# Building the second-level factors of w_out from row-block pairs in the first token group, instead of from reloaded quarters in groups 1 and 2

## The chip, the core and the metric

The kernel runs on one core of a Trainium2 chip. The metric is the time of one execution of the whole program on the device, in microseconds (us), and the median of several runs is compared. The engines of a core run side by side, each in its own program order, and meet through semaphores: TensorE (PE) multiplies, VectorE (DVE) and ScalarE (ACT) work element by element, GpSimd (POOL) and SyncE (SP) here do little but issue DMA transfers, which 16 DMA engines carry out.

## The reference, cut to what matters

```python
B, H, S, D = 4, 8, 768, 64                      # attention, blocks of 64 positions
intra = einsum('bhic,bhjc->bhij', qb, kb) * Dmask
out[:, :, sl] = einsum('bhij,bhjd->bhid', intra, vb) + einsum('bhid,bhde->bhie', qb * lam_pow, kv_state)
kv_state = lam_block * kv_state + einsum('bhsd,bhse->bhde', kb * rev_pow, vb)
...
x = out.transpose(0, 2, 1, 3).reshape(3072, 512)
h = x @ w_in                                    # 512 x 2048
g = h - np.tanh(h)
return (g @ w_out).astype(np.float32)           # 2048 x 512
```

The weights reach the kernel as 64-bit floats, q, k and v as 32-bit floats. It rounds the weights to 32-bit floats itself, block by block.

## The kernel before

**Tokens and weights.** Six groups (g = 0 to 5) of 512 tokens pass through attention, the product with `w_in` (`up`), the function g = h - tanh(h) and the product with `w_out` (`down`). The matrices are cut in halves both ways, and from group 1 on a product of two such 2x2 block matrices is made by Strassen's scheme in Winograd's form, with 7 products in place of 8: product n (1 to 7) multiplies one sum of blocks of g by one factor, which is a block of `w_out` or a sum of blocks. The seven factors are B11, B21, B22 and T1 to T4. Each of the seven can be cut a second time in the same way: its 16 matmuls of 128x256 columns ("plain", function `down`, line 655) become 7 times 4 matmuls of 128x128 columns ("twice", function `down_twice`, line 708). The set `TWICE = (3, 5, 6, 4, 7)` names the products that are made twice; each needs the seven sub-factors of its factor, again blocks and sums of blocks, now of 128 columns.

**Where the factors live.** `w_out` has 16 row blocks of 128 rows. Row blocks kt and kt + 8 form pair kt (kt = 0 to 7). In group 0, `round_block` rounds the two 64-bit blocks of a pair (three ACT instructions, then a shift and an add on DVE, lines 279 to 284), and `sums_out(kt)` makes T1, T2, T3 and T4 of the pair (lines 255 to 258) and writes all seven factors to a DRAM tensor `factors`. The sub-factors live in a second DRAM tensor, `fine`, with 5 factors times 7 sub-factors. Those sub-factors that are plain blocks (numbers 1, 2 and 3) are copied there by `sums_out` too. A sum sub-factor adds rows of pair 2u to rows of pair 2u + 1.

**The first group.** Group 0 does its `down` plainly by pairs: `down_first(kt)` makes 14 matmuls for the seven products of pair kt, into seven PSUM accumulators that stay open over all eight pairs. While pair kt is multiplied, pair kt + 1 is summed and pair kt + 3 is rounded into the buffer that pair kt leaves (three buffers in turn: two tiles `wt`, and the tensors `ws[3]` and `ws[2]`). `sums_late(kt)` overwrites two blocks of g with their sums, between products 1, 2 and the other five. Raw 64-bit blocks are loaded by POOL's queue into four buffers (`WAHEAD = 4`), so a load waits until an earlier raw block has been rounded.

**The sums of the sub-factors, before.** They are made in groups 1 and 2. `load_quarters(t)` reads four quarters of a factor back from `factors`, `factors_twice(t)` makes the four sums (lines 602 to 604) and writes each to `fine`. Factors of products 5 and 6 are made in group 1's `up`, those of 4, 7 and 3 in group 2's `up`. So in group 1 products 4, 7 and 3 are plain (line 550). The quarters of group 2 pass through the same ring of seven buffers `wb` (`RING = 7`) that brings the factors of all products, in the order of the list `stream`.

**What sets the order.** Each engine carries out its instructions in the order that a scheduler gives them, and those marked with `tc.keep_in_program_order` (or `tied`) keep the order of the text among themselves. A DMA that POOL issues waits in POOL's own queue, and all that stands behind it waits too. SP loads q, k and v; for group 2 on it loads q and k in 16 small transfers each (`load_blocks`, line 143), and the first of these waits until the last raw block has been rounded, since its buffer takes the place of the raw blocks.

Of the kernel before, what the change touches and what calls it, by code (L numbers as in the profile page):

```python
# [24 lines left out]
def kernel(  # L25
# [154 lines left out]

    NX = 7
    factors = dram.tile([NX, 128, KH, 256], F32, name="factors")

# [38 lines left out]
    def weights(n):  # L222

        while ready["done"] < min(n, len(blocks)):
            at_ = ready["done"]
            load_weights(at_ + WAHEAD)
            kind, n_, m = blocks[at_]
            if kind == "out" and m == 0:
                pair[n_] = pair_tiles(n_)
            w = w1[n_][:, m] if kind == "in" else pair[n_][0][:, 2 * m:2 * m + 2]  # L230
            if at_ in wraw:
                round_block(w, wraw.pop(at_), at_ < 2 * KI)
            else:
                load_block(nc.gpsimd, w, kind, n_, m)
            ready["done"] += 1

    def pair_tiles(kt):

        if kt % 3 == 2:
            return tuple(ws[u].rearrange("p x k c -> p (x k) c")[:, 0:4] for u in (3, 2))  # L240
        wt = wst.tile([128, 8, 256], F32, name="wt", tag="w")
        return wt[:, 0:4], wt[:, 4:8]

# [7 lines left out]
    def sums_out(kt):  # L251
        bt, tt = pair[kt]
        b11, b12, b21, b22 = (bt[:, x] for x in range(4))
        t1, t2, t4, t3 = (tt[:, x] for x in range(4))
        nc.vector.tensor_tensor(t1, b12, b11, op=AL.subtract)
        nc.vector.tensor_tensor(t2, b22, t1, op=AL.subtract)
        nc.vector.tensor_tensor(t3, b22, b12, op=AL.subtract)
        nc.vector.tensor_tensor(t4, b21, t2, op=AL.subtract)
        f = factors[:].rearrange("x p k c -> p x k c")
        nc.gpsimd.dma_start(out=f[:, 0:1, kt, :], in_=bt[:, 0:1, :])  # L260
        nc.gpsimd.dma_start(out=f[:, 1:3, kt, :], in_=bt[:, 2:4, :])
        nc.gpsimd.dma_start(out=f[:, 3:NX, kt, :], in_=tt[:, 0:4, :])

        for x, j in ((1, 0),) if kt % 2 == 0 else ((2, 0), (3, 1)):
            dst = fine[:, SUB.index(x), :, kt // 2, :].rearrange("n p c -> p n c")
            nc.gpsimd.dma_start(out=dst[:, 0:1], in_=bt[:, 3:4, ts(j, 128)])
            nc.gpsimd.dma_start(out=dst[:, 1:5], in_=tt[:, 0:4, ts(j, 128)])

    def round_block(w, raw64, first):
# [12 lines left out]

        tied(first, nc.vector.tensor_scalar(out=wb, in0=wb, scalar1=3, scalar2=None, op0=AL.logical_shift_left))
        nc.vector.tensor_tensor(wi, wi, add, op=AL.add)  # L284

# [263 lines left out]
    def twice(g, n):  # L549
        return n in TWICE and not (g == NG - 1 and n == 3) and not (g == 1 and n in (4, 7, 3))  # L550

# [7 lines left out]
    def pieces_of(g):  # L559
        if g >= GI:  # L560
            yield from ((g, ("in", 4), x) for x in (6, 5, 3))
        if g == 2:
            yield from ((g, ("quarter", t), x) for t in (2, 3, 4) for x in range(4))
        for n in (1, 2, 4, 5, 6, 7):
            yield from ((g, n, x) for x in (SUB if twice(g, n) else range(NU)))
        if g == NG - 1:
            yield from ((g, 3, x) for x in range(NU))
            return
        for kind, x in in_turn(g):
            if kind == "down":  # L570
                yield g, 3, x
            elif x in (3, 5, 6):
                yield g + 1, ("in", 2), x
# [3 lines left out]

    MADE = (5, 6, 4, 7, 3)
    quarters = {}

    def quarter_source(t, i, j):
        return factors[XAT[FACT[MADE[t]][1]]].rearrange("p (u m) c -> p u m c", m=2)[:, :, i, ts(j, 128)]

    def load_quarters(t):

        for i in range(2):
            for j in range(2):
                if t > 1:
                    quarters[t, i, j] = piece(2, ("quarter", t), 2 * i + j).rearrange("p m (v c) -> p (m v) c", v=2)
                    continue  # L590
                if t == 0:
                    x = late["pool"].tile([128, NU, 128], F32, name="wq", tag="wb", bufs=RING)
                else:
                    x = opool.tile([128, NU, 128], F32, name="oq", tag="o")
                nc.gpsimd.dma_start(out=x, in_=quarter_source(t, i, j))
                quarters[t, i, j] = x

    def factors_twice(t):

        b11, b12, b21, b22 = (quarters.pop((t, i, j)) for i in range(2) for j in range(2))  # L600
        t1, t2, t4 = (late["pool"].tile([128, NU, 128], F32, name=f"wt{x}", tag="sums", bufs=4) for x in (1, 2, 4))
        for x, dst, a, b in ((5, t1, b12, b11), (6, t2, b22, t1), (7, b12, b22, b12), (4, t4, b21, t2)):
            tc.keep_in_program_order(nc.vector.tensor_tensor(dst, a, b, op=AL.subtract))
            nc.gpsimd.dma_start(out=fine[TWICE.index(MADE[t]), SUB.index(x)], in_=dst)
            yield

    def piece(g, n, x):

        i = stream.index((g, n, x))
        while sent["n"] < min(i + RING, len(stream)):  # L610
            g_, n_, x_ = stream[sent["n"]]
            t = late["pool"].tile([128, 2, 256], F32, name="wb", tag="wb", bufs=RING)
            if isinstance(n_, tuple) and n_[0] == "quarter":
                nc.gpsimd.dma_start(out=t.rearrange("p m (v c) -> p (m v) c", v=2),
                                    in_=quarter_source(n_[1], *divmod(x_, 2)))
            elif isinstance(n_, tuple):
                nc.gpsimd.dma_start(out=t.rearrange("p m c -> p (m c)"), in_=fine_in[
# [157 lines left out]
    ACC = {1: ("ya", 1), 2: ("w", 1), 5: ("z", 1), 6: ("yb", 1), 7: ("att", 4), 4: ("att", 4), 3: ("att", 4)}  # L775
    FIRST = {1: (11, 0, 0), 2: (21, 0, 2), 3: (21, 0, 3), 4: (22, 1, 2), 5: ("S1", 1, 0), 6: (11, 1, 1), 7: (12, 1, 3)}

# [5 lines left out]
    def down_first(kt, ns):  # L783

        u, m = divmod(kt, 2)
        for n in ns:
            if kt == 0:
                acc[n] = bank("acc", *ACC[n]).rearrange("q (m c) -> q m c", m=2)
            c, part, x = FIRST[n]
            a, b = hidden(0, c)[:, u, m], pair[kt][part][:, x]  # L790
            for r in range(2):
                nc.tensor.matmul(out=acc[n][:, r, :], lhsT=a[:, ts(r, 128)], rhs=b, start=kt == 0 and r == 0,  # L792
                                 stop=kt == KH - 1, skip_group_check=True)

    def sums_late(kt):
        u, m = divmod(kt, 2)
        g11, g21, s1 = (hidden(0, c)[:, u, m] for c in (11, 21, "S1"))
        nc.vector.tensor_tensor(g11, s1, g11, op=AL.subtract)
        nc.vector.tensor_tensor(g21, g21, g11, op=AL.subtract)

    def first_results():
        flat = {n: t.rearrange("q m c -> q (m c)") for n, t in acc.items()}
        q, o11, q5, o12 = (otile(x) for x in ("q1", "o11", "q5", "o12"))
        nc.scalar.activation(q, flat[1], AF.Copy)
        nc.vector.tensor_tensor(o11, q, flat[2], op=AL.add)
        store(0, 11, o11)
        nc.vector.tensor_tensor(q, q, flat[6], op=AL.add)
        nc.vector.tensor_tensor(q5, q, flat[5], op=AL.add)
        nc.vector.tensor_tensor(q, q, flat[7], op=AL.add)
        nc.vector.tensor_tensor(o12, q5, flat[3], op=AL.add)  # L810
        store(0, 12, o12)
        nc.vector.tensor_tensor(q, q, flat[4], op=AL.add)
        store(0, 21, q)
        nc.vector.tensor_tensor(q5, q5, flat[7], op=AL.add)
        store(0, 22, q5)
# [58 lines left out]
    weights(NU * KI + 6)  # L874
    run(p1[4:])
    for kt in range(KH):
        down_first(kt, (1, 2))
        if kt + 1 < KH:
            sums_out(kt + 1)
        sums_late(kt)  # L880
        down_first(kt, (5, 4, 7, 6, 3) if kt + 1 < KH else (5, 6, 7, 4, 3))
        if kt + 3 < KH:
            weights(ready["done"] + 2)
        if kt == 2:
            sums_in(1)
# [5 lines left out]

    turns = {1: (0, ((0, 7), (1, 14))), 2: (7 * NU, ((2, 1), (3, 5), (4, 9)))}
    made, making = [], {}
    load_quarters(0)
    load_quarters(1)
    up(1, 0, 1)
    for g in range(1, NG):
        last = g == NG - 1
        p0, p1 = attention(g + 1) if not last else ([], [])
        for u in range(NU):  # L900
            for n in (2, 6, 5, 7, 1, 4, 3) if g < GI else (1, 7, 3) if u == 0 else (6, 5, 1, 7, 3) if u + 1 < NU else (
# [7 lines left out]
                if g == 1 and u < 2 and n == 5:  # L909
                    sums_in(u + 2)  # L910
                if g in turns:
                    made.append(n)
                    step = len(made) - turns[g][0]
                    for t, first in turns[g][1]:
                        if step == first:
                            if t > 1:
                                load_quarters(t)
                            making[t] = factors_twice(t)
                        if first <= step < first + 4:
                            next(making[t])  # L920
            if g == GI - 1:
# [68 lines left out]
```

## Time and profile before

| what | value |
|---|---|
| runs | 670.99, 670.28, 668.80 us; median 670.28 us |
| profiled execution, its own time | 669.39 us |
| its span, first to last instruction | 667.6 us |
| PE busy in the span | 655.6 us (98%), 4920 matmul records |
| DVE, ACT, POOL busy | 466.4, 213.7, 210.8 us |
| group 0's `down` (98.53 to 147.0 us) | PE busy all of it, DVE 30.5 us, DMA busy share 0.81 |
| group 1's `up` and `down` | 147.0 to 263.4 us |
| group 2's `up` and `down` | 263.4 to 369.7 us |
| DMA through POOL's queue | 96.49 MB, 45.0% of 16 engines' span |

A matmul on 32-bit data leaves two records in the trace, so "x32" in a line of the PE timeline is 16 matmuls. A record's duration overlaps its neighbours', so the time of a stretch is read from the start of one row to the start of the next. In a timeline, the columns are start (us from the span's start), duration, engine, line, operation, output<-inputs, shape, count, and in brackets the idle time before and what ended it.

### The profile page before, as it was taken

How to read it: one execution, taken by the hardware profiler on the slowest of the kernel's cores; microseconds unless marked ns; L12 is line 12 of the kernel's file. 1: busy time of each engine (PE TensorE's matmuls, PEld its weight loads, DVE VectorE, ACT ScalarE, POOL GpSimd, SP SyncE). 2: the span in 40 equal slices, each digit the busy share in tenths (PEclk: the TensorE clock that was granted, in tenths of full speed). 3: DMA queues.
4: the chain of work that ended last, by engine and by line, in shares of the span. 5: the costliest groups of instructions: out<-in, count | busy, mean ns of one | idle time of the engine just before them, and what ended most of it. 6: DMA issues, size and time to landing. Idle time of an engine off the chain costs nothing.

```text
span 667.6 us, 13061 instructions
## 1 busy us (share of the span) xinstructions
PE 655.6 (98%) x4920; PEld 594.1 (89%) x4920; DVE 466.4 (70%) x839; ACT 213.7 (32%) x402; POOL 210.8 (32%) x365
## 2 busy tenths in 40 slices
PE   7899999999999999999999999999999999999998
PEld 6688888888888989888999988999988899988897
DVE  4467896746988762599885379987368877357753
ACT  4787935503321112341112343112233112234110
POOL 0001445734522433254436101344300245400251
PEclk9999999999999999999999999999999999999999
DMA  9999988958855977568889533698730677610495
GB/s 209 223 201 261 286 306 234 342 160 233 229 133 137 235 188 205 150 198 259 239 260 280 142 76 75 170 274 255 215 70 17 158 237 219 219 37 0 120 295 170
DMA packets 163038, 128.82 MB, mean 193 GB/s; under 512 B 134176, under 2 KB 135328, under 8 KB 162976
## 3 DMA queue, kind: packets, MB, share of 16 engines
q0 software_dynamic: 29296, 96.49, 45.0%
q1 hardware_dynamic: 133536, 31.50, 24.0%
q8 instruction: 39, 0.64, 0.4%
q14 instruction: 23, 0.19, 0.1%
q10 hardware_dynamic: 144, 0.00, 0.0%
HBM read 103.55 MB, written 24.38 MB: 192 GB/s over the span
## 4 chain that ended last, share of the span: by engine, by line
PE 79%; issue 9%; DMA 5%; POOL 2%; SPq 2%; ACT 1%; DVE 1%; DVEq 0%; POOLq 0%; ACTq 0%
PE y L446 12%; PE y L708 10%; PE acc L792 7%; PE zw L708 7%; PE h L763 7%; PE z L446 7%; PE w L655 4%; PE y L655 4%; PE y L530 4%; PE plain L655 3%; PE sp L340 3%; PE op L394 3%; PE z L530 2%; DMA wb<-fine 2%; PE op L388 1%
## 5 line engine op out<-in xcount | busy, mean ns | idle before, releaser
L620 POOL DMA_DIRECT2D wb<-fine x147 | 79.4, 541 | 113.7 <-PE y L708 50.6
L623 POOL DMA_DIRECT2D wb<-factors x56 | 30.4, 543 | 155.9 <-PE y L655 99.7
L454 ACT ACTIVATE th<-g 128x512 f32<-128x512 f32 x76 | 47.7, 632 | 99.1 <-DVE g L459 33.2
L446 PE MATMUL y<-xt,w 128*128 128x256 f32 x320 | 74.0, 380 | 0.0
L446 PEld LDWEIGHTS y<-xt,w 128*128 128x128 f32 x320 | 59.9, 190 | 8.5 <-ACT g L534 0.9
L711 ACT ACTIVATE q<-y 128x128 f32<-128x128 f32 x84 | 23.3, 278 | 130.8 <-PE y L708 130.0
L455 DVE TENSOR_TENSOR g<-g,th 128x512 f32<-128x512 f32 x76 | 51.9, 688 | 16.8 <-ACT th L454 16.7
L763 PE MATMUL h<-xt,w 128*128 128x256 f32 x256 | 58.0, 383 | 2.3 <-DVE w L284 2.3
L763 PEld LDWEIGHTS h<-xt,w 128*128 128x128 f32 x256 | 47.7, 190 | 10.2 <-DVE w L284 2.6
L708 PE MATMUL y<-wb,g 128*128 128x128 f32 x384 | 51.1, 278 | 0.0
L708 PEld LDWEIGHTS y<-wb,g 128*128 128x128 f32 x384 | 46.4, 192 | 1.1 <-issue 0.3
L446 PE MATMUL z<-tt,ws 128*128 128x256 f32 x160 | 38.0, 380 | 0.0
L446 PE MATMUL z<-xt,ws 128*128 128x256 f32 x160 | 37.9, 380 | 0.0
L446 PE MATMUL y<-tt,ws 128*128 128x256 f32 x160 | 37.8, 379 | 0.0
L655 PE MATMUL y<-wb,g 128*128 128x256 f32 x160 | 35.6, 379 | 0.7 <-DVE g L465 0.7
L655 PE MATMUL w<-wb,g 128*128 128x256 f32 x160 | 35.8, 382 | 0.0
L344 DVE TENSOR_TENSOR ss<-sp,mask 128x512 f32<-128x512 f32 x48 | 31.1, 684 | 6.3 <-PE sp L340 6.3
L205 POOL DMA_DIRECT2D raw<-in_moe_w_out_dram x16 | 8.8, 549 | 84.7 <-ACT r L281 66.2
L655 PEld LDWEIGHTS y<-wb,g 128*128 128x128 f32 x160 | 30.3, 190 | 5.1 <-PE y L446 1.0
L446 PEld LDWEIGHTS z<-xt,ws 128*128 128x128 f32 x160 | 30.3, 190 | 4.3 <-ACT g L462 0.2
L655 PEld LDWEIGHTS w<-wb,g 128*128 128x128 f32 x160 | 30.1, 190 | 4.4
L708 PE MATMUL zw<-wb,g 128*128 128x128 f32 x256 | 33.8, 275 | 0.0
(198 smaller groups left out, 1349.6 us busy)
## 6 DMA issues: line engine op xcount, KB each, us to landing
wb<-fine POOLq DMA_DIRECT2D x147, 256.0 KB, 4.0
wb<-factors POOLq DMA_DIRECT2D x68, 256.0 KB, 4.2
raw<-in_moe_w_out_dram POOLq DMA_DIRECT2D x16, 512.0 KB, 5.8
v_nat<-in_v_dram SPq DMA_DIRECT2D x24, 256.0 KB, 5.2
fine<-wt POOLq DMA_DIRECT2D x24, 256.0 KB, 4.7
wb<-fine_in POOLq DMA_DIRECT2D x24, 256.0 KB, 4.2
k_nat<-in_k_dram SPq DMA_DIRECT2D x20, 256.0 KB, 4.9
raw<-in_moe_w_in_dram SPq DMA_DIRECT2D x8, 512.0 KB, 6.5
```

What stands on the lines that cost most here:

```text
L344: tied(g == 0, nc.vector.tensor_tensor(ss[:, j], sp[j], mask[:, j], op=AL.mult))
L446: nc.tensor.matmul(out=t[:, m, :], lhsT=wt[:, kt, ts(m, 128)], rhs=x[:, kt, :], start=first and m == 0 and kt == 0, stop=kt == 1, skip_gro ...
L454: nc.scalar.activation(th, src, AF.Tanh)
L455: nc.vector.tensor_tensor(dst(c), src, th, op=AL.subtract)
L530: nc.tensor.matmul(out=dst[:, ts(u, 128)], lhsT=a, rhs=b, start=x in (1, 2, 5) and u == 0, stop=True, skip_group_check=True)
L620: nc.gpsimd.dma_start(out=t.rearrange("p m c -> p (m c)"), in_=fine[TWICE.index(n_), SUB.index(x_)].rearrange("p u c -> p (u c)"))
L623: nc.gpsimd.dma_start(out=t, in_=factors[XAT[FACT[n_][1]]][:, 2 * x_:2 * x_ + 2, :])
L655: nc.tensor.matmul(out=t[:, m, :], lhsT=a[:, u, kt, ts(m, 128)], rhs=wb[:, kt, :], start=first and u == 0 and m == 0 and kt == 0, stop=u = ...
L708: nc.tensor.matmul(out=dst, lhsT=a[:, u, :], rhs=wb[:, ts(u, 128)], start=x in (1, 2) and u == 0, stop=u == NU - 1, skip_group_check=True)
L711: nc.scalar.activation(keep, dst, AF.Copy)
L763: tied(u == 0, nc.tensor.matmul(out=hm[c][:, m, :], lhsT=w1[u][:, i, a, ts(m, 128)], rhs=xt[0, t][:, i, :], start=m == 0 and i == 0, stop= ...
L792: nc.tensor.matmul(out=acc[n][:, r, :], lhsT=a[:, ts(r, 128)], rhs=b, start=kt == 0 and r == 0, stop=kt == KH - 1, skip_group_check=True)
```

## The change

Nothing changes in what is computed: the same 35 sub-factors reach `fine`.

- The quarters go: `load_quarters`, `factors_twice`, their place in `stream` and in the loop over groups are removed. `factors` keeps three of its seven members (`NX = 3`: B11, B21, B22), since no one reads the others any more.
- `sums_fine(u)`, new, runs in group 0 after `sums_out(2u + 1)`. It makes the four sums of all five factors for one pair of pairs: eight DVE instructions (128x128 and 128x512) and eight DMAs. Its results go into buffers of the attention stage that lie idle then (tags "qd", "qt", "kt").
- The pair's tile is laid out anew, in a part `x` with B11, B12 and a part `y` with the other six, so that one DMA can write five sub-factors side by side.
- `sums_late(kt + 1)` now runs during pair kt and writes to a tile of its own (tag "th") instead of over g.
- Product 4, 7 and 3 are made twice in group 1 too.
- DVE's order in group 0 is fixed by the text: sums, late sums, `sums_fine`, rounding of pair kt + 3. `sums_in(1)` moves from pair 2 to pair 5, and the results of group 0 come after `sums_fine(3)`.

```diff
-    NX = 7
+    NX = 3
...
     def sums_out(kt):
-        bt, tt = pair[kt]
-        b11, b12, b21, b22 = (bt[:, x] for x in range(4))
-        t1, t2, t4, t3 = (tt[:, x] for x in range(4))
-        nc.vector.tensor_tensor(t1, b12, b11, op=AL.subtract)
...
+        x, y = pair[kt]
+        b11, b12, b21, b22, t1, t2, t4, t3 = (t[:, i] for t, n in ((x, 2), (y, 6)) for i in range(n))
+        for dst, a, b in ((t1, b12, b11), (t2, b22, t1), (t3, b22, b12), (t4, b21, t2)):
+            tied(kt > 0, nc.vector.tensor_tensor(dst, a, b, op=AL.subtract))
...
-        nc.gpsimd.dma_start(out=f[:, 1:3, kt, :], in_=bt[:, 2:4, :])
-        nc.gpsimd.dma_start(out=f[:, 3:NX, kt, :], in_=tt[:, 0:4, :])
...
+        nc.gpsimd.dma_start(out=f[:, 1:NX, kt, :], in_=y[:, 0:2, :])
+
+        for n, j in ((1, 0),) if kt % 2 == 0 else ((2, 0), (3, 1)):
+            nc.gpsimd.dma_start(out=fine[:, SUB.index(n), :, kt // 2, :].rearrange("n p c -> p n c"),
+                                in_=y[:, 1:6, ts(j, 128)])
+
+    def sums_fine(u):
+
+        (b11, b12), (b21, b22) = (tuple(pair[2 * u + i][1][:, 1:6, ts(j, 128)] for j in range(2)) for i in range(2))
+        one = work.tile([128, 4, 1, 128], F32, name="f1", tag="qd")
+        parts = [(0, 1, [one[:, x] for x in range(4)]),
+                 (1, 5, [work.tile([128, 4, 128], F32, name="f4", tag=t) for t in ("qt", "kt") * 2])]
+        for x, a, b in ((5, b12, b11), (6, b22, 5), (7, b22, b12), (4, b21, 6)):
+            for lo, hi, t in parts:
+                dst = {5: t[0], 6: t[1], 7: t[2], 4: t[3]}
+                tc.keep_in_program_order(nc.vector.tensor_tensor(
+                    dst[x], a[:, lo:hi], dst[b] if isinstance(b, int) else b[:, lo:hi], op=AL.subtract))
+                nc.gpsimd.dma_start(out=fine[lo:hi, SUB.index(x), :, u, :].rearrange("n p c -> p n c"), in_=dst[x])
...
-        return n in TWICE and not (g == NG - 1 and n == 3) and not (g == 1 and n in (4, 7, 3))
+        return n in TWICE and not (g == NG - 1 and n == 3)
...
-        if g == 2:
-            yield from ((g, ("quarter", t), x) for t in (2, 3, 4) for x in range(4))
...
     def sums_late(kt):
         u, m = divmod(kt, 2)
         g11, g21, s1 = (hidden(0, c)[:, u, m] for c in (11, 21, "S1"))
-        nc.vector.tensor_tensor(g11, s1, g11, op=AL.subtract)
-        nc.vector.tensor_tensor(g21, g21, g11, op=AL.subtract)
+        s24[kt] = work.tile([128, 2, HB], F32, name="s24", tag="th")
+        tc.keep_in_program_order(nc.vector.tensor_tensor(s24[kt][:, 0], s1, g11, op=AL.subtract))
+        tc.keep_in_program_order(nc.vector.tensor_tensor(s24[kt][:, 1], g21, s24[kt][:, 0], op=AL.subtract))
...
+    sums_late(0)
     for kt in range(KH):
-        down_first(kt, (1, 2))
+        down_first(kt, (1, 2, 5, 4, 7, 6, 3) if kt + 1 < KH else (1, 2, 6, 5, 7, 3, 4))
         if kt + 1 < KH:
             sums_out(kt + 1)
-        sums_late(kt)
-        down_first(kt, (5, 4, 7, 6, 3) if kt + 1 < KH else (5, 6, 7, 4, 3))
+            sums_late(kt + 1)
+        if kt % 2 == 0:
+            sums_fine(kt // 2)
         if kt + 3 < KH:
             weights(ready["done"] + 2)
-        if kt == 2:
+        if kt == 5:
             sums_in(1)
     first_results()
```

More of the change, by code (lines that the diff above doesn't have):

```diff
@@ L229, in weights @@
                 pair[n_] = pair_tiles(n_)
-            w = w1[n_][:, m] if kind == "in" else pair[n_][0][:, 2 * m:2 * m + 2]
+            w = w1[n_][:, m] if kind == "in" else pair[n_][m][:, 0:2]
             if at_ in wraw:
@@ L239, in pair_tiles @@
         if kt % 3 == 2:
-            return tuple(ws[u].rearrange("p x k c -> p (x k) c")[:, 0:4] for u in (3, 2))
+            x, y = (ws[u].rearrange("p x k c -> p (x k) c") for u in (3, 2))
+            return x[:, 0:2], y[:, 0:6]
         wt = wst.tile([128, 8, 256], F32, name="wt", tag="w")
-        return wt[:, 0:4], wt[:, 4:8]
+        return wt[:, 0:2], wt[:, 2:8]
     def sums_in(u):
@@ L251, in sums_out @@
     def sums_out(kt):
-        bt, tt = pair[kt]
-        b11, b12, b21, b22 = (bt[:, x] for x in range(4))
-        t1, t2, t4, t3 = (tt[:, x] for x in range(4))
-        nc.vector.tensor_tensor(t1, b12, b11, op=AL.subtract)
-        nc.vector.tensor_tensor(t2, b22, t1, op=AL.subtract)
-        nc.vector.tensor_tensor(t3, b22, b12, op=AL.subtract)
-        nc.vector.tensor_tensor(t4, b21, t2, op=AL.subtract)
-        f = factors[:].rearrange("x p k c -> p x k c")
-        nc.gpsimd.dma_start(out=f[:, 0:1, kt, :], in_=bt[:, 0:1, :])
@@ L261, in sums_out @@
-        nc.gpsimd.dma_start(out=f[:, 1:3, kt, :], in_=bt[:, 2:4, :])
-        nc.gpsimd.dma_start(out=f[:, 3:NX, kt, :], in_=tt[:, 0:4, :])
[L264 to L267, printed above, removed]
+        x, y = pair[kt]
+        b11, b12, b21, b22, t1, t2, t4, t3 = (t[:, i] for t, n in ((x, 2), (y, 6)) for i in range(n))
@@ new lines, in sums_out @@
+        for dst, a, b in ((t1, b12, b11), (t2, b22, t1), (t3, b22, b12), (t4, b21, t2)):
+            tied(kt > 0, nc.vector.tensor_tensor(dst, a, b, op=AL.subtract))
+        f = factors[:].rearrange("x p k c -> p x k c")
+        nc.gpsimd.dma_start(out=f[:, 0:1, kt, :], in_=x[:, 0:1, :])
+        nc.gpsimd.dma_start(out=f[:, 1:NX, kt, :], in_=y[:, 0:2, :])
+        for n, j in ((1, 0),) if kt % 2 == 0 else ((2, 0), (3, 1)):
+            nc.gpsimd.dma_start(out=fine[:, SUB.index(n), :, kt // 2, :].rearrange("n p c -> p n c"),
+                                in_=y[:, 1:6, ts(j, 128)])
@@ L281, in round_block @@
         tied(first, nc.scalar.activation(halves[:, :, 1], hif, AF.Copy, scale=2.0 ** -60))
-        tied(first, nc.vector.tensor_scalar(out=wb, in0=wb, scalar1=3, scalar2=None, op0=AL.logical_shift_left))
-        nc.vector.tensor_tensor(wi, wi, add, op=AL.add)
+        late_block = ready["done"] >= NU * KI + 6
+        tied(first or late_block, nc.vector.tensor_scalar(out=wb, in0=wb, scalar1=3, scalar2=None,
+                                                          op0=AL.logical_shift_left))
+        tied(late_block, nc.vector.tensor_tensor(wi, wi, add, op=AL.add))
     def bank(name, tag, bufs):
@@ L576 @@
     sent = {"n": 0}
[L578 to L605, printed above, removed]
     def piece(g, n, x):
@@ L612, in piece @@
             t = late["pool"].tile([128, 2, 256], F32, name="wb", tag="wb", bufs=RING)
[L613 to L616, printed above, removed]
+            if isinstance(n_, tuple):
                 nc.gpsimd.dma_start(out=t.rearrange("p m c -> p (m c)"), in_=fine_in[
@@ L775 @@
     ACC = {1: ("ya", 1), 2: ("w", 1), 5: ("z", 1), 6: ("yb", 1), 7: ("att", 4), 4: ("att", 4), 3: ("att", 4)}
-    FIRST = {1: (11, 0, 0), 2: (21, 0, 2), 3: (21, 0, 3), 4: (22, 1, 2), 5: ("S1", 1, 0), 6: (11, 1, 1), 7: (12, 1, 3)}
+    FIRST = {1: (11, 0, 0), 2: (21, 1, 0), 3: ((1,), 1, 1), 4: (22, 1, 4), 5: ("S1", 1, 2), 6: ((0,), 1, 3), 7: (12, 1, 5)}
     def sums_first(u):
@@ L789, in down_first @@
             c, part, x = FIRST[n]
-            a, b = hidden(0, c)[:, u, m], pair[kt][part][:, x]
+            a = hidden(0, c)[:, u, m] if isinstance(c, (int, str)) else s24[kt][:, c[0]]
+            b = pair[kt][part][:, x]
             for r in range(2):
@@ L793, in down_first @@
                                  stop=kt == KH - 1, skip_group_check=True)
+    s24 = {}
     def sums_late(kt):
@@ L804, in first_results @@
         nc.scalar.activation(q, flat[1], AF.Copy)
-        nc.vector.tensor_tensor(o11, q, flat[2], op=AL.add)
+        tc.keep_in_program_order(nc.vector.tensor_tensor(o11, q, flat[2], op=AL.add))
         store(0, 11, o11)
[L807 to L810, printed above, removed]
+        tc.keep_in_program_order(nc.vector.tensor_tensor(q, q, flat[6], op=AL.add))
+        tc.keep_in_program_order(nc.vector.tensor_tensor(q5, q, flat[5], op=AL.add))
+        tc.keep_in_program_order(nc.vector.tensor_tensor(q, q, flat[7], op=AL.add))
+        tc.keep_in_program_order(nc.vector.tensor_tensor(o12, q5, flat[3], op=AL.add))
         store(0, 12, o12)
-        nc.vector.tensor_tensor(q, q, flat[4], op=AL.add)
+        tc.keep_in_program_order(nc.vector.tensor_tensor(q, q, flat[4], op=AL.add))
         store(0, 21, q)
-        nc.vector.tensor_tensor(q5, q5, flat[7], op=AL.add)
+        tc.keep_in_program_order(nc.vector.tensor_tensor(q5, q5, flat[7], op=AL.add))
         store(0, 22, q5)
@@ L889 @@
     late["pool"] = ctx.enter_context(tc.tile_pool(name="late", bufs=1))
[L892 to L895, printed above, removed]
     up(1, 0, 1)
@@ L910 @@
                     sums_in(u + 2)
[L911 to L920, printed above, removed]
             if g == GI - 1:
```

## The prediction

> **What bounds the kernel now.** First the page: PE, and the chain that ended last.
>
> ```profile
> PE 655.6 (98%) x4920; PEld 594.1 (89%) x4920; DVE 466.4 (70%) x839; ACT 213.7 (32%) x402; POOL 210.8 (32%) x365
> ...
> PE 79%; issue 9%; DMA 5%; POOL 2%; SPq 2%; ACT 1%; DVE 1%; DVEq 0%; POOLq 0%; ACTq 0%
> ```
>
> PE is idle for 12 us of 667.6. So work taken off another engine is worth nothing; a change pays by fewer PE microseconds, or by removing a wait of PE, and it costs where it makes PE wait. Second, the PE timeline of groups 1 to 4.
>
> ```profile
> 215.28 7.17 PE L655 MATMUL plain<-wb,g 128*128 128x256 f32 x32
> 222.29 1.05 PE L708 MATMUL y<-wb,gS 128*128 128x128 f32 x8
> ...
> 228.64 2.06 PE L340 MATMUL sp<-qt,kt 64*128 64x128 f32 x32
> ...
> 298.23 0.67 PE L655 MATMUL y<-wb,g 128*128 128x256 f32 x2 [0.67 <-DVE g L465]
> ...
> 323.44 1.16 PE L708 MATMUL y<-wb,g 128*128 128x128 f32 x8
> ...
> 336.73 2.06 PE L340 MATMUL sp<-qt,kt 64*128 64x128 f32 x32
> ...
> 436.12 1.16 PE L708 MATMUL y<-wb,gS 128*128 128x128 f32 x8 [0.76 <-DMA wb<-fine]
> ```
>
> From start to start, plain product 4 of group 1 takes 222.29 - 215.28 = 7.01 us and product 5, made twice, 228.64 - 222.29 = 6.35 us. Two products made twice in a row (group 2, 4 and 5) take 336.73 - 323.44 = 13.29, where 12.70 would do, and group 3 shows the reason: PE waits for a factor's DMA. The third row is PE's wait in group 2's `up`, behind the quarters.
>
> Third, the stretch windows of group 0's `down`, and the transfers in it. Columns: stretch, its length, then busy time (and instructions) of PE, PEld, DVE, ACT and POOL, PE's clock, the DMA share, GB/s.
>
> ```profile
> 116.60:122.70 6.10, 6.10 (x30) 5.38 (x29) 4.43 (x11) 3.32 (x5) 3.73 (x6) 1.00 0.98 336
> 122.70:128.70 6.00, 6.00 (x30) 5.28 (x29) 5.09 (x14) 4.08 (x6) 5.34 (x8) 1.00 1.01 374
> ...
> raw<-in_moe_w_out_dram POOLq DMA_DIRECT2D x16, 512.0 KB, 5.8
> ```
>
> DVE's timeline gives the prices of sums:
>
> ```profile
> 130.44 0.69 DVE L284 CUSTOM_DVE_ANT_0 wt<-wt,r 128x1024 uint16<-128x1024 uint16 x1
> 131.04 0.42 DVE L283 TENSOR_SCALAR wt<-wt 128x512 uint32<-128x512 uint32 x1
> 131.37 0.42 DVE L799 TENSOR_TENSOR g<-g,g 128x256 f32<-128x256 f32 x1
> 131.71 0.68 DVE L284 CUSTOM_DVE_ANT_0 wt<-wt,r 128x1024 uint16<-128x1024 uint16 x1
> ...
> 165.64 0.29 DVE L503 TENSOR_TENSOR ws<-w 128x128 f32<-128x128 f32 x1
> 165.84 0.69 DVE L455 TENSOR_TENSOR g<-g,th 128x512 f32<-128x512 f32 x1
> ```
>
> Each stretch is one pair, 14 matmuls in 6.05 us. PE never waits there, though DVE and POOL are far in use and the DMA engines full; that is where the new work goes. DVE rows follow each other closer than their durations: a 128x256 sum each 0.335 us, a 128x512 or an add of the rounding each 0.60, a 128x128 each 0.20, a shift each 0.34, and 0.46 where one 128x256 sum reads the one before.
>
> **What it takes off the path.** Products 4, 7 and 3 of group 1: three times 7.01 - 6.35 = 0.66, so -1.98 us. Group 2's `up`, from 263.40 to 312.47, takes 49.07; group 3's, which has no quarters, 417.87 - 369.73 = 48.14: -0.93 us (0.67 is the wait shown, the rest smaller gaps beside it). The 20 sums, 20 reloads and 20 writes of the quarters (20 x 0.60 = 12 us of DVE, some 22 us of POOL at 0.55 each) come off no path otherwise: in group 1's `up`, 147.15 to 192, PE is busy 44.85 of 44.85 us already. The longer evacuations of three products made twice lie on DVE and ACT, which have 8.0 and 22.2 us idle of the 26.1 from 215.35 on; without that cover they would cost the 0.6 us that I charge for group 1 again.
>
> **What it adds in group 1.** Five products made twice follow each other, 35 pieces of 256 KB where 14 fine and 12 plain ones went. The pair 4 and 5 cost 13.29 in group 2, 442.57 - 428.84 = 13.73 in group 3 and 546.77 - 533.75 = 13.02 in group 4, over 12.70: +0.32 to +1.03; I take +0.6, the middle of the three.
>
> **What it adds in group 0.** DVE gets 4 x 8 sums of `sums_fine`: 4 x 4 x (0.60 + 0.20) = 12.8 us, to 30.5 of 48.5 us: it fits, but in a fixed order. POOL gets 32 DMAs of 0.55 (128x128) and 0.75 (128x4x128), and loses the write of four factors (0.79) and the small copies (0.55 each); a copy of five sub-factors is not in the trace, between 0.75 (four) and 1.3 (four and one apart), and I take 0.82, near the first. Per two pairs that is 2 x (0.55 + 0.72) + 3 x 0.82 + 4 x (0.55 + 0.75) + 4 raw loads x 0.54 = 12.4 us in 12.1 us. So POOL's queue, 25 us busy before, has no slack, and the raw loads stand in it behind `sums_fine`'s writes. I followed the new order by these durations from 101.15 us (first late sum), with T0 = 104.58 the end of pair 0 on PE and 6.05 us for each further pair:
> - `sums_fine(0)` on DVE 104.3 to 107.5; pair 3 rounded to 109.6, pair 4 to 114.0. POOL issues two copies from 103.6 and the eight writes to 110.4, then raw blocks 11, 12 and 13 up to 113.1.
> - `sums_out(3)` ends 115.5, `sums_fine(1)` runs 116.3 to 119.5 and pair 5 is rounded to 121.6. POOL has pair 3's four DMAs to 117.2 and the eight writes to 122.4; raw block 14, the second half of pair 6, is issued only then and lands 122.4 + 5.8 = 128.2.
> - DVE stands at pair 6's second shift from 125 on: ACT converts it to 128.8 and two more steps of 0.64 to 130.1, the add ends 130.7. Behind it in DVE's fixed order stands T1 of pair 5: ready 131.1. PE wants it at T4 + 1.73 = 128.79 + 1.73 = 130.5 (after products 1 and 2). PE waits 0.6, and 0.3 more for T4 of that pair.
> - `sums_fine(2)` then ends 136.2, pair 7 is rounded to 138.3, T1 of pair 6 is ready 138.7: PE, which has product 1 of pair 7 in between, waits 0.4, then 0.3.
>
> Sum: +1.6 us. The row of raw loads has 3.5 to 7.4 us to landing. At 4.5 the same steps leave 0.2 us; at 7.4 PE waits 2.5 for pair 5 and 0.7 for pair 6: +3.2. Past the row's longest, at 9, it would be near +5.
>
> Also moved: the results of group 0 start behind `sums_fine(3)`, at 148.6 instead of 143.2. Their first reader, product 2 of group 1, needs its bank 1.73 us after product 1 begins (150.3): hidden by 1 us. SP's first small loads start with the last rounding, 138.3 instead of 132.5; before, the second k block had been issued by 172 for transposes at 191.6, so 6 us are covered. The late sums a block ahead and `sums_in(1)` at pair 5 cost nothing while DVE keeps these times.
>
> **The skill on it.** "DMA: Bandwidth & Descriptors", section "Anatomy of one DMA — SWDGE (gpsimd) path", gives a DMA issued by GpSimd 2.0 us plus its bytes over 436e3: for a 512 KB raw block an estimate of 3.2 us; by that alone group 0 would lose nothing and the kernel gain 2.3 us. The trace has a median of 5.8 for the same thing, with the DMA engines full, and decides. The page's section "Issuing engines are not separate DMA queues" speaks against the change: all queues share 16 engines, so writes moved into a full stretch delay the loads in it. The window at 1.01 agrees that there is little room.
>
> **The sum.** -1.98 - 0.93 + 0.6 + 1.6 = -0.7 us on the profiled 669.39. That execution is 0.9 under the median of 670.28; on the median it makes 669.6 us. By bounds: -2.91 + 0.32 + 0 = -2.6 (667.7) to -2.91 + 1.03 + 5 = +3.1 (673.4).
>
> **The rivals.** *Faster, 667.9* (-2.4): the raw blocks land in about 4.5 us, as POOL sat waiting and the DMA share was 0.51 in the pair from 104.5 to 110.6, room for `sums_fine(0)`; only ring waits of 0.3 and 0.2 remain. Against: block 14 falls in the full stretch after 122. *Slower, 672.9*: one mechanism, the raw blocks 14 to 16 late behind `sums_fine`'s writes. By bytes the stage's POOL traffic goes from 10.62 MB (63.6% of 48.5 us) to some 13.9 (five pairs lose 512 KB of factors each, 2.6 MB; 5.1 MB of sums and 1 MB of copies come): 40 us of DMA time in 47, with SP's on top. If landing then takes 9 us or more, +5 - 2.4 = +2.6. It decides from a landing of about 8.5 us, beyond the longest row. *That group 1 gains nothing*, its ring starved by five products in a row: it would need 2 us of new waits on top, where group 3 shows 1.03: 671.6, within no change.
>
> **How the numbers follow.** This kernel's runs spread by 2.2 us, so 0.3% (2.0 us) is what can be told from none: 668.3 to 672.3 counts as the same. Forecast, a small loss of group 0 that eats most of the gain: 0.46. Faster: 0.28. Slower: 0.26, group 1's failure within the forecast's band. The likeliest one's own range is 668.3 to 671.5; taking in the bounds of both sides, 667.4 to 672.8.
>
> **What would show it.** PE's product 4 and 5 of group 1 in 13.0 to 13.7 us; group 2's `up` near 48.1; in group 0's `down` waits of PE named after DVE's sum of pair 5 and 6, with ACT before them waiting for a raw DMA issued near 122. No such wait would make the forecast too high by 1.6; PE waiting already at pairs 2 to 4, or on anything in group 1's `up`, would make it wrong.

## The result and the profile after

The changed kernel takes 671.18 us against 669.58 us (medians of 22 runs each): a ratio of 1.0028, with a 95% interval of 1.0016 to 1.0040. It is slower by 1.6 us where the prediction had it faster by 0.7. The page of the changed kernel (engines; shares of the chain that ended last; the raw blocks' loads, KB each and median us from issue to landing):

```profile
PE 655.7 (98%) x4992; PEld 594.7 (89%) x4992; DVE 480.3 (72%) x869; ACT 215.1 (32%) x413; POOL 198.9 (30%) x346
...
PE 70%; issue 10%; DMA 8%; POOL 4%; DVE 3%; ACT 2%; SPq 2%; POOLq 0%; DVEq 0%; ACTq 0%
...
raw<-in_moe_w_out_dram POOLq DMA_DIRECT2D x16, 512.0 KB, 5.7
```

PE is as busy as before (655.6 us), in a longer span: 670.4 us, 672.15 us of own time. DMA, POOL and DVE have grown in the chain (5%, 2% and 1% before): PE waits more. Where, the PE timelines of both kernels tell, from the first row of one stage to the first row of the next (worked out from their start times, in us):

| stage | before | after | difference | predicted |
|---|---|---|---|---|
| up to group 0's `down` | 98.53 | 99.90 | +1.37 | 0 |
| group 0's `down` | 48.45 | 52.43 | +3.98 | +1.6 |
| group 1 | 116.42 | 115.24 | -1.18 | -1.98 + 0.6 = -1.38 |
| group 2's `up` | 49.07 | 48.14 | -0.93 | -0.93 |
| group 2's `down` | 57.26 | 56.79 | -0.47 | 0 |
| all that follows | 297.9 | 297.9 | 0.0 | 0 |

The first row need not be the change: in the profiles of the experiments, whose work up to there is nearly the same, group 0's `down` begins anywhere from 97.91 to 99.62. Without it the two executions differ by 1.4 us, near the 1.6 of the medians. The loss sits in one stage. The PE timeline of the changed kernel there, and in group 1:

```profile
130.22 1.89 PE L770 MATMUL acc<-ws,g 128*128 128x256 f32 x8
134.71 1.13 PE L770 MATMUL acc<-ws,gS 128*128 128x256 f32 x4 [2.60 <-DVE ws L256]
...
142.46 1.13 PE L770 MATMUL acc<-wt,gS 128*128 128x256 f32 x4 [0.31 <-DVE wt L256]
...
220.63 1.16 PE L685 MATMUL y<-wb,g 128*128 128x128 f32 x8
...
227.35 1.06 PE L685 MATMUL y<-wb,gS 128*128 128x128 f32 x8
...
232.59 1.16 PE L685 MATMUL zw<-wb,gS 128*128 128x128 f32 x8 [0.61 <-DVE gS L690]
```

Eight records of 128x256 take 1.73 us, so the second row should have begun at 131.95: pair 5 loses 2.76 us, waiting for T1 (`ws L256`), and pair 6 loses 0.47 at the third row. Both are the waits that the prediction named; the first is 2.76 where it had 0.6. The way back from it leads over DVE and ACT (their timelines in the same kernel)

```profile
126.37 0.69 DVE L295 CUSTOM_DVE_ANT_0 wt<-wt,r 128x1024 uint16<-128x1024 uint16 x1
132.35 0.43 DVE L293 TENSOR_SCALAR wt<-wt 128x512 uint32<-128x512 uint32 x1 [5.29 <-ACT wt L288]
133.63 0.69 DVE L295 CUSTOM_DVE_ANT_0 wt<-wt,r 128x1024 uint16<-128x1024 uint16 x1 [0.86 <-ACT r L290]
134.24 0.88 DVE L256 TENSOR_TENSOR ws<-ws 128x256 f32<-128x256 f32 x2
```

```profile
112.58 1.21 ACT L288 ACTIVATE wt<-raw 128x512 f32<-128x512 f32 x2
...
131.65 0.67 ACT L288 ACTIVATE wt<-raw 128x512 f32<-128x512 f32 x1 [6.52 <-DMA raw<-in_moe_w_out_dram]
```

to POOL's timeline:

```profile
117.62 1.77 POOL L262 DMA_DIRECT2D fine<-wt  x2 [1.46 <-DVE wt L256]
119.39 1.85 POOL L276 DMA_DIRECT2D fine<-f  x3
122.03 2.58 POOL L276 DMA_DIRECT2D fine<-f  x4 [0.79 <-DMA factors<-wt]
124.78 0.75 POOL L276 DMA_DIRECT2D fine<-f  x1 [0.17 <-issue]
125.52 1.09 POOL L205 DMA_DIRECT2D raw<-in_moe_w_out_dram  x2
```

DVE stands idle for 5.3 us at the rounding of pair 6 while the sum that PE wants, whose inputs are long there, stands behind it in DVE's order. ACT has nothing to convert, because raw block 14 (the first of the two loads in the last row) was issued at 125.52 behind the eight writes of `sums_fine(1)` (L276). Its buffer had been free since about 113.8, when ACT had converted pair 4 (the first ACT row). In the kernel before the same block was issued at 114.47, 15.9 us from the stage's start, where it now is 25.6.

### The profile page after: what moved, and what is told of

Read it like the earlier page. It is cut to its first block, busy times and chain, and to the rows that moved or that the text cites. A ratio compares the mean times of both kernels' runs of the same rounds, so it can differ in the third digit from the quotient of the medians.

```text
span 670.4 us, 13235 instructions
## 1 busy us (share of the span) xinstructions
PE 655.7 (98%) x4992; PEld 594.7 (89%) x4992; DVE 480.3 (72%) x869; ACT 215.1 (32%) x413; POOL 198.9 (30%) x346
## 4 chain that ended last, share of the span: by engine, by line
PE 70%; issue 10%; DMA 8%; POOL 4%; DVE 3%; ACT 2%; SPq 2%; POOLq 0%; DVEq 0%; ACTq 0%
PE y L457 13%; PE y L685 10%; PE z L457 8%; PE zw L685 7%; PE h L740 5%; PE w L632 4%; PE y L632 4%; PE y L541 4%; PE sp L351 3%; DMA raw<-in_moe_w_in_dram 2%; PE op L405 2%; POOL wb L597 2%; DMA raw<-in_moe_w_out_dram 2%; PE z L541 2%; DMA wb<-fine 2%
## 5 line engine op out<-in xcount | busy, mean ns | idle before, releaser
L597 POOL DMA_DIRECT2D wb<-fine x168 | 90.5, 539 | 138.3 <-PE y L685 60.4
L688 ACT ACTIVATE q<-y 128x128 f32<-128x128 f32 x96 | 26.7, 278 | 150.0 <-PE y L685 149.2
L600 POOL DMA_DIRECT2D wb<-factors x44 | 23.7, 541 | 167.0 <-PE y L632 127.8
L685 PE MATMUL y<-wb,g 128*128 128x128 f32 x456 | 60.6, 278 | 0.0
L685 PEld LDWEIGHTS y<-wb,g 128*128 128x128 f32 x456 | 55.1, 192 | 1.3 <-issue 0.3
L685 PE MATMUL zw<-wb,g 128*128 128x128 f32 x304 | 40.3, 275 | 0.1
L685 PEld LDWEIGHTS zw<-wb,g 128*128 128x128 f32 x304 | 37.0, 192 | 0.3 <-DVE g L690 0.3
L632 PEld LDWEIGHTS y<-wb,g 128*128 128x128 f32 x160 | 30.4, 190 | 4.1
```

Of the source, the lines that this page charges most:

```text
L600: nc.gpsimd.dma_start(out=t, in_=factors[XAT[FACT[n_][1]]][:, 2 * x_:2 * x_ + 2, :])
L632: nc.tensor.matmul(out=t[:, m, :], lhsT=a[:, u, kt, ts(m, 128)], rhs=wb[:, kt, :], start=first and u == 0 and m == 0 and kt == 0, stop=u = ...
L685: nc.tensor.matmul(out=dst, lhsT=a[:, u, :], rhs=wb[:, ts(u, 128)], start=x in (1, 2) and u == 0, stop=u == NU - 1, skip_group_check=True)
L688: nc.scalar.activation(keep, dst, AF.Copy)
```

## The experiments

Each changes the changed kernel. Four theories: **A**, the raw block's place in POOL's queue; **B**, DVE's load of 32 new sums; **C**, the bytes in a stretch where the DMA engines are full; **D**, formed after e1 to e4, a late input and DVE's fixed order in series. The results together ("issue" is raw block 14's from the stage's start; "group 1" from its `up` to that of group 2; these three are each of one profiled execution; times are medians; ratios are against the kernel before, run again beside each experiment with medians from 669.92 to 670.25, with 95% intervals):

| kernel | issue | group 0's `down` | group 1 | time | ratio |
|---|---|---|---|---|---|
| before | 15.9 | 48.45 | 116.42 | 669.58 | |
| changed | 25.6 | 52.43 | 115.24 | 671.18 | 1.0028 [1.0016, 1.0040] |
| e1 raw blocks on SP | 13.9 | 50.58 | 115.23 | 668.95 | 0.9981 [0.9966, 0.9997] |
| e2 a raw block ahead of the writes | 19.4 | 52.71 | 115.38 | 669.32 | 0.9992 [0.9973, 1.0012] |
| e3 writes on SP | 15.2 | 55.72 | 125.20 | 683.59 | 1.0204 [1.0185, 1.0222] |
| e4 writes cut in two | 34.6 | 60.65 | 115.35 | 681.48 | one run |
| e5 e1, w_out's sums a pair earlier | 15.4 | 48.77 | 117.61 | 667.61 | 0.9961 [0.9948, 0.9974] |
| e6 w_out's sums a pair earlier | 28.7 | 53.52 | 115.20 | 671.02 | 1.0016 [1.0002, 1.0030] |
| e7 e5, transposes later | 15.4 | 48.56 | 115.30 | 666.23 | 0.9945 [0.9927, 0.9963] |
| e8 transposes later | 26.7 | 53.45 | 114.33 | 669.94 | 0.9994 [0.9977, 1.0011] |
| e9 no new sums on DVE | 24.7 | 56.58 | 115.20 | 675.25 | one run |
| e10 half the writes, same bytes | 23.8 | 58.24 | 115.19 | 675.60 | 1.0097 [1.0066, 1.0129] |
| e11 all sums a pair earlier | 29.9 | 51.76 | 115.95 | 670.25 | 1.0005 [0.9992, 1.0018] |
| e12 all moves | 16.2 | 48.45 | 115.72 | 665.98 | 0.9936 [0.9917, 0.9955] |

### The late raw block: its place in the queues

**e1.** The last six raw blocks leave POOL's queue.

```diff
-                load_block(nc.sync if block[0] == "in" else nc.gpsimd, raw64, *block, block[0] == "in")
+                load_block(nc.sync if block[0] == "in" or ready["loaded"] >= NU * KI + 10 else nc.gpsimd, raw64, *block, block[0] == "in")
```

> The last six raw blocks of w_out (the seventh block of pair 5 on) are issued by SP instead of POOL; nothing else moves. Theory A, the place in POOL's queue: the 2.76 us that PE lost at pair 5 came from a raw block that stood behind eight writes until 125.5 us. On SP it is issued when its buffer comes free, near 114, and lands near 120: ACT no longer waits 6.5 us, PE's waits in group 0's stage fall from 3.8 us in sum to under 0.5, the stage from 52.4 to about 48.6, the time to about 667.5. Theory B, DVE's fixed order with 12.8 us of new sums: PE's waits on the late sums stay above 2 us, 671. Theory C, DMA engines too full: the blocks land more than 9 us after issue and 1 to 3 us of wait remain, 669 to 671.

Pair 5's wait is gone, as theory A had it, and the time falls by some 0.5% of the changed kernel's. But pair 6 now loses 1.76 us (its row of the PE timeline of e1):

```profile
139.19 1.13 PE L770 MATMUL acc<-wt,gS 128*128 128x256 f32 x4 [1.59 <-DVE wt L256]
```

T1 of pair 6 stands on DVE behind the rounding of pair 7. That rounding needs the tile of pair 4, which is held by pair 4's copy to `fine`, and POOL issued this copy at 128.82, again behind the eight writes:

```profile
128.82 0.86 POOL L262 DMA_DIRECT2D fine<-wt  x1 [0.79 <-DVE wt L293]
```

It landed at 135.74, and ACT starts to convert pair 7 at 135.88. (The other thing that ACT waits for by the program, the third step of `sums_fine(2)`, had ended at 134.2.) The queue's place decides twice, once for a load and once for a buffer's release.

**e2.** One raw block is issued before each set of writes, `load_weights(ready["done"] + WAHEAD)` ahead of `sums_fine(kt // 2)`.

> One raw block is issued by POOL ahead of each set of eight small writes, not behind it; all transfers and their engine stay. Theory A: the block that came too late is issued near 119.5 instead of 125.5 and lands near 125.5, just before DVE reaches it at 127: the wait of 2.6 us at pair 5 is gone, pair 6 may keep 0.3 to 0.5; stage 48.6 to 49.3, time 667.5 to 668.3. Theory B: waits as before, 671. Theory C: the block still lands after 9 us, waits of 1 to 2 us, 669 to 670.

Block 14 goes out at 118.86 and lands before 126.5. Pair 5's wait is gone. Now block 16 is the late one, issued at 130.61 and converted from 136.73 on; pair 6 waits 2.09 us, and then comes something that no theory had. Two rows of e2's PE timeline, and a stretch window (start:end, length, busy time of PE, PEld, DVE, ACT, POOL, PE's granted clock, DMA share, GB/s):

```profile
139.83 1.13 PE L770 MATMUL acc<-wt,gS 128*128 128x256 f32 x4 [2.09 <-DVE wt L256]
140.96 3.63 PE L770 MATMUL acc<-wt,g 128*128 128x256 f32 x8
```

```profile
141.00:144.40 3.40, 3.40 (x8) 2.77 (x9) 3.33 (x7) 0.00 (x0) 3.22 (x5) 0.52 1.00 285
```

After the wait PE runs at half clock for 3.4 us, and the eight records take 3.46 us, not 1.73: a wait of 2.09 us costs 3.8.

**e3.** The 32 writes go to SP (`nc.sync.dma_start` in `sums_fine`).

> The 32 writes of the new sums are issued by SP instead of POOL; the raw blocks stay on POOL. Theory A: POOL's queue loses 5.2 us for each two pairs, the late block is issued near 117.5 and lands near 123.5; no wait at pair 5, stage about 48.6, time about 667.5. Theory B: waits as before, 671. Theory C: as many bytes in the same stretch, so waits of 1 to 3 us stay, 669 to 671.

A miss: 12 us slower than the changed kernel. What theory A named did come: block 14 is issued at 113.45, lands at 121.59, and pair 5 doesn't wait. But SP's queue is no free place (its timeline; then its 32 issues as a group, with the shortest, median and longest in ns):

```profile
104.21 49.88 SPq L276 DMA_DIRECT2D fine<-f  x32
154.19 0.81 SPq L131 DMA_DIRECT2D k_nat<-in_k_dram  x1
...
L276 SPq DMA_DIRECT2D fine<-f x32: 332/652/4743, 104.2 to 153.4; - x32
```

The row spans 49.9 us because the writes wait in it for their sums, the last of which DVE makes from 147.37 on; one issue takes 0.65 us in the median, but one took 4.74. In the full stretch the writes land late: DVE waits 5.44 us for a temporary whose write was issued at 109.92 and landed at 125.01, and PE waits 4.02 us at pair 4. (In the changed kernel no write of the sums took more than 5.3 us to land; why it is longer from SP isn't shown.) Behind the writes in SP's order stand the loads of q and k: those in sixteen parts begin at 168.6, not at 142.1, and PE pays 8.03 us in group 1, where a transpose lacks its input.

**e4.** Each write is cut into two of 64 partitions, a dose for theory A without a byte more.

> Each of the 32 writes of the new sums is cut in two by partitions (64 of them are issued); bytes, sums and order stay. Theory A: POOL's queue grows by 8 issues of about 0.5 us, 4 us for each two pairs, so the late block is issued 4 to 6 us later and PE's wait at pair 5 grows from 2.6 to 6 or more; time 675 or more. Theories B and C: the same sums and the same bytes, so no change from 671 to 672.

Block 14 is issued at 133.99, 8.9 us later from the stage's start, and PE waits 7.07 us for the rounding of the pair itself and 2.2 us elsewhere: the stage is 8.2 us longer. Time in POOL's queue, without a byte more, can make the loss. (Not all of it is issue: this set takes 12.15 us, and in 2.75 of them POOL waits, mostly until earlier DMAs have landed.)

### Sums or bytes

**e9.** The 32 sums are left out and the writes read the pair's tile (`in_=a[:, lo:hi]`).

> The changed kernel without the 32 new sums on DVE: the same 32 writes take the raw parts of w_out (so the second-level factors of groups 1 on are not computed). Theory A, POOL's queue: raw block 14 is still issued behind the writes, near 122 to 125, PE keeps a wait of 1 to 2.7 us at pair 5, stage 50 to 52. Theory B, DVE's load: with 3.2 us less work for each two pairs the waits are gone, stage 48.5.

The wait at pair 5 is still 1.67 us without one of the new sums, and ACT waits for block 14 as before (rows of PE and ACT):

```profile
132.08 1.13 PE L768 MATMUL acc<-ws,gS 128*128 128x256 f32 x4 [1.67 <-DVE ws L256]
```

```profile
129.01 0.67 ACT L286 ACTIVATE wt<-raw 128x512 f32<-128x512 f32 x1 [2.06 <-DMA raw<-in_moe_w_out_dram]
```

So DVE's load (B) isn't needed for the wait; that it adds something to it isn't ruled out. The stage says nothing of the rest, since the writes now hold the pair's tile until they land, so that ACT waits 5.01 and 4.74 us for `fine`'s DMAs before it can convert the next pair.

**e10.** The sums stay on DVE but aren't written to `fine`; four writes of 320 KB from the pair's tile replace the eight, with the same bytes.

```diff
-                nc.gpsimd.dma_start(out=fine[lo:hi, SUB.index(x), :, u, :].rearrange("n p c -> p n c"), in_=dst[x])
+            nc.gpsimd.dma_start(out=fine[0:5, SUB.index(x), :, u, :].rearrange("n p c -> p n c"), in_=a)
```

> The changed kernel with all sums on DVE, but four writes of 320 KB for each two pairs in place of eight of 64 and 256 KB: the same bytes in half the issues (they take the raw parts of w_out, so the second-level factors of groups 1 on are not written). Theory A: POOL's queue loses 8 x 0.65 - 4 x 0.885 = 1.7 us and the wait for a DMA that is still in flight for each two pairs; raw block 14 is issued 2 to 3 us earlier, PE's 2.76 us at pair 5 fall to under 1, stage 49 to 50.3, time 668 to 669.5. Theory C, bytes: no change, 671.

A miss of theory A, and the most telling one. POOL's and ACT's timelines of e10:

```profile
121.98 1.11 POOL L205 DMA_DIRECT2D raw<-in_moe_w_out_dram  x2
```

```profile
130.27 0.66 ACT L288 ACTIVATE wt<-raw 128x512 f32<-128x512 f32 x1 [2.55 <-DMA raw<-in_moe_w_out_dram]
```

The block is issued 1.8 us earlier from the stage's start (121.98 - 98.16 = 23.8 against 25.6) but lands no earlier (130.25 - 98.16 = 32.1 against 131.63 - 99.90 = 31.7): it takes 8.3 us. The same bytes stand ahead of it, and the engines are full. So C has a part: in this stretch a load lands when the bytes issued ahead of it are through. The landings in the other traces agree. In the changed kernel, e4, e6 and e8 to e11, block 14 takes from 4.8 to 8.3 us, but it lands from 2.6 to 3.4 us after the last write ahead of it (131.63 after 128.45 in the changed kernel, 130.25 after 126.83 here, 128.98 after 126.03 in e9). e1 and e2 helped because they moved the block ahead of the writes' bytes; e10 only moved it closer behind them. (That pair 6 waits another 2.65 us here is the held tile of e9 again.)

### The order on DVE

**e5** adds to e1 that the four sums of a pair, with their copies, come a pair earlier in the program, and so before the rounding of the pair that follows it:

```diff
+    sums_out(1)
...
-        if kt + 1 < KH:
-            sums_out(kt + 1)
+        if kt + 2 < KH:
+            sums_out(kt + 2)
+        if kt + 1 < KH:
             sums_late(kt + 1)
```

> The last six raw blocks on SP as before, and the four sums of each pair (and with them its copies on POOL) a pair earlier, so that on DVE they stand ahead of the rounding of the pair after next and not behind it. Theory D, the loss has two links in series, a late input (raw block, or pair 7's buffer that waits for a copy behind the writes in POOL's queue) and DVE's fixed order, which puts a sum that needs nothing of it behind the rounding of that input: the 1.6 us wait at pair 6 that was left goes too, group 0's stage is 48.5 to 49, time 665 to 666.5. Theory A alone (only the queue place matters): the wait at pair 6 stays, as pair 7 is no earlier, 668 to 669.

No wait is left in the stage: 48.77. But group 1 has become 2.4 us longer. Rows of its PE timeline:

```profile
228.35 1.13 PE L685 MATMUL y<-wb,gS 128*128 128x128 f32 x8 [0.84 <-DMA wb<-fine]
230.76 1.13 PE L685 MATMUL zw<-wb,gS 128*128 128x128 f32 x8 [1.29 <-DMA wb<-fine]
```

PE now waits for the sub-factors' DMAs, which from 200 to 235 us take 5.6 us in the median against 4.5 in the changed kernel. e7 has nearly the same group 0, a median of 5.4 and only 0.23 us of such a wait, so what decides this share isn't shown.

**e6** makes the same move without SP.

> Only the sums a pair earlier; the raw blocks stay on POOL behind the writes. Theory D: the late raw block still comes near 131, but no sum that PE waits for stands behind it; pair 6's own first product needs the block near 137, when it is rounded: wait under 1 us in sum, time 665.5 to 668. Theory A alone: the block is as late as before, so the wait of 2 to 3 us stays somewhere, 670 to 671.

Another miss, with a reason that fits. T1 to T4 no longer stand behind the late block, so the late sums of g do (DVE's and PE's timelines of e6):

```profile
135.54 1.55 DVE L256 TENSOR_TENSOR wt<-wt 128x256 f32<-128x256 f32 x4
137.00 0.42 DVE L779 TENSOR_TENSOR s<-gS,g 128x256 f32<-128x256 f32 x1
```

```profile
137.48 3.48 PE L770 MATMUL acc<-ws,s 128*128 128x256 f32 x8 [2.78 <-DVE s L779]
```

PE starts as soon as the late sum of pair 5 ends, and then runs at half clock: the eight records take 3.31 us. **e11** moves these as well, with a third buffer from the resting ring "ss" (`sums_late(kt + 2)` beside `sums_out(kt + 2)`).

> The changed kernel with both kinds of sums that PE waits for, those of w_out's pairs and the late ones of g, a pair earlier (a third buffer for the late sums from a ring that rests); the raw blocks stay on POOL behind the writes, and nothing of the eight writes is changed. Theory D: the raw block of pair 6 is as late as before (it lands near 131), but nothing that pair 5 needs stands behind its rounding: no wait at pair 5, at most 0.5 us where pair 6 itself begins and up to 1.5 us at pair 7, whose rounding now follows late; stage 48.6 to 50.5, time 667 to 669. Theory A alone: a wait of 2 to 3 us stays, stage 51.5 to 53, time 670 to 671.

The two waits of pair 5 are gone, though block 14 is issued later than in the changed kernel (129.48, 29.9 us from the stage's start), and pair 6 starts 0.33 us late. The delay comes out at pair 7 (PE waits 1.26, 0.25 and 0.67 us there), and the stage is only 0.7 us shorter, which group 1 gives back: with group 0's results later on DVE, its second product waits 0.49 us for them. So the order on DVE decides which pair pays for a late block, and only a block that comes earlier takes the bill away: order alone 0.7 us, queue alone 1.85 us (e1), both 3.66 us (e5) of 3.98.

### Group 1, and all together

**e8** leaves group 0 and moves the attention's transposes, `run(p1[0:1])`, from ahead of product 5 to behind its first two pieces.

> The changed kernel with only the transposes of the attention moved behind the first two pieces of product 5. Group 1's product 5 took 7.22 us with a wait of 0.61 for DVE's difference behind those transposes. If DVE's order is the whole cause, product 5 falls to 6.6 us and group 1 from 115.24 to about 114.6, time about 0.6 under the changed kernel. If the factors' DMAs are the next bound right behind it, DVE's wait goes but waits for a factor's DMA of as much take its place: group 1 115.0 to 115.4, time unchanged within 0.3 us.

The row that waited 0.61 us follows the one before it without a gap (two rows of e8's PE timeline), and no DMA wait takes its place: products 4 and 5 take 13.03 us, not 13.94, and group 1 114.33. The first reading holds.

```profile
230.22 1.06 PE L685 MATMUL y<-wb,gS 128*128 128x128 f32 x8
231.11 1.06 PE L685 MATMUL zw<-wb,gS 128*128 128x128 f32 x8
```

**e7** puts this on e5, and **e12** adds e11's late sums.

> As the first of these three, and in each group from the second on the attention's transposes are issued behind the first two pieces of product 5 made twice, not ahead of it, so that DVE's difference for that product stands in front of the six transposes. If group 1's wait of 0.61 us is DVE's order, it goes: product 5 of group 1 from 7.22 to about 6.6 us and the whole 0.3 to 0.7 under the first of these three. If it is a factor's DMA (the ring), it stays, and the time is that of the first within 0.3 us.

> All moves together: raw blocks on SP, both kinds of sums a pair earlier, the attention's transposes behind the first pieces of product 5. Group 0's stage has no wait to lose beyond the version with the late sums in place (48.56), so 48.5 to 48.7; time 665.5 to 667, under both kernels. Were the late sums still a hidden limit in that version, it would be 0.5 us or more lower than it.

e7's group 1 is 2.3 us under e5's, more than the 0.61 us of the transposes can give; most of it are the DMA waits that e5 had. e12 has group 0's `down` at 48.45, the value of the kernel before, and is 0.64% faster than that kernel: what the change cost in group 0 is given back. Not all of that gain need belong to the change, since the transposes move in every group from the second on, and this move wasn't tried on the kernel before. Between e7 and e12 the intervals don't tell a difference.

## Why the prediction was wrong

**The bound, and what comes off the path: right.** Product 4 of group 1 went from 7.01 to 6.72 us, what follows product 5 there fell by 1.76 us (1.32 was counted for 7 and 3), and group 2's `up` fell by 0.93 us to the 48.14 us of group 3. In addition products 4 and 5 of group 2 went from 13.29 to 12.82 us. I had counted nothing there; that the quarters no longer pass through the ring is a likely reason, and wasn't tried.

**"+0.6" for group 1: size nearly right by luck, cause wrong.** Net of the gain it was 1.98 - 1.18 = 0.8 us. By the prediction's own measure, products 4 and 5 over 12.70, it was 13.94 - 12.70 = 1.24, outside its 0.32 to 1.03; the products behind gained more than counted. I took it for waits on the ring and its DMAs, and said that the longer evacuations were covered by 8.0 us of idle DVE. In the changed kernel DVE is busy for 24.5 of the 26.1 us from 220.63 on, and its timeline shows the difference of product 5 (L690) right behind the last of six attention instructions:

```profile
231.28 0.65 DVE L341 TENSOR_TENSOR qd<-qt,fwd 128x512 f32<-128x512 f32 x1
231.85 0.68 DVE L690 TENSOR_TENSOR gS<-gS,s 128x512 f32<-128x512 f32 x1
```

Idle time summed over 26 us was no cover for an instruction with one due time. e8 shows the cause of 0.91 of the 1.24; the ring showed only in e5, e7 and e12 (1.29, 0.23 and 0.56 us at most in one wait).

**"+1.6" for group 0: the step that failed.** The mechanism was the one on record: block 14 behind the writes, DVE at pair 6's shift, T1 behind it, PE late at pair 5 and then at pair 6, even the three small waits (0.27, 0.47, 0.27 against 0.3, 0.4, 0.3). The term was mis-sized at "issued only then", 122.4: 23.9 us from the stage's start by my steps, 25.6 measured. Of this difference of 1.75 us, 0.8 arose before the writes: DVE ended the sums of pair 3 about 0.4 later than I had reckoned, POOL, which waited 1.46 us for them, began 0.3 after that, and the two copies took 0.89 us each and not 0.82. Another 0.9 arose within them: POOL waited 0.79 us at a write until an earlier DMA had landed. By the traces it is the eighth before it: that one landed 0.52 us before the write began, here (121.51 and 122.03) as in e2 (121.23 and 121.76) and e11 (125.13 and 125.65). I had POOL issue without limit. With 0.3 us more for landing (6.1 against 5.8) the sum is 2.05, and 0.6 + 2.05 is near the 2.76 measured. There was no slack left in any of the three links, so each such piece went to PE in full. My upper bound of 5 for this term held the 3.98. The half clock that most timed runs show (last section) had no term at all; the profiled execution has none in this stage, and the three timed runs at full clock have a median of 670.95 us, 1.4 over the kernel before.

**The rivals.** "Faster" fails with the landing of 6.1 us. "Slower", with its price, needed landings of 8.5 us; the path was the same, but the lateness came mostly from the issue. (The bytes of its sum add up to 14.1 MB, not 13.9; the stage moved 12.57 MB through POOL's queue.) e10 shows that landing and issue can't be priced apart when the engines are full.

**Two queues, one set of engines.** I set the estimate of 3.2 us from the Trainium skill's page "DMA: Bandwidth & Descriptors" aside and kept what its section "Issuing engines are not separate DMA queues" says, that all queues share 16 engines. e1 agrees: with the raw blocks on SP, the second set of eight writes on POOL took 7.0 to 8.8 us to land, against 3.0 to 5.2 in the changed kernel. The same section says that issuing from several engines saves only the sequencer's time, usually small beside the DMA itself. Here eight issues take 5.2 us of POOL, near the 5.7 us in which a raw block lands, and the 1.85 us that e1 gained in the stage come from the block's place: it no longer stands behind them.

## What to carry to other kernels

When writes are added to a queue that also carries loads, find the next load behind them and follow it to the first instruction that waits for it, and then what stands behind that one in each engine's fixed order: the price is paid by whatever stands there, often something that needs nothing of the load. A load must be moved ahead of the bytes, not only ahead of the issues, when the DMA engines are full. And cover is a matter of due times: idle time summed over a stage hides nothing that an engine's order has put behind other work.

## What the runs showed of the hardware

**A wait of PE can be charged twice.** After idle stretches of 2.09 us (e2), 2.77 us (e8) and 2.78 us (e6) PE ran at half clock for about 3.4 us, which costs 1.7 us more. It doesn't always happen: after 2.60 us in the changed kernel's profile, and 1.59 us in e1's, the clock stayed at 1.00. A stretch of 3.4 us at half clock in 670 us makes a mean of 0.9975, and 16 of the 22 timed runs of the changed kernel have a mean granted clock of 0.997 or 0.995; for e2 the runs at 0.997 have a median of 670.89 us, those at 1.000 of 669.01; for the changed kernel it is 671.65 and 670.95, but its four runs at 0.995 have 670.88, so its times don't show the loss clearly. The Trainium skill, "TensorE: Matmul & The Clock Gate", section "What's actually happening", has a free-running window of about 3.4 us and half clock after at least one idle window. The length agrees; but here 2.1 us of idle were enough, so a window need not be idle from end to end.

**An issue can last on SP.** The same 32 writes took POOL 0.55 to 0.83 us each (5.24 us for eight, where none waited). On SP (e3) the median was 0.65 us, but in the full stretch one issue took 4.74.
